# A delta-rule attention and mixture-of-experts kernel: the key products of the first two chunks over four other PSUM banks and all tiles of the array, and a planner with new prices

## The chip, the core and the metric

The kernel runs on one core of a Trainium2 chip. The metric is the device time of one execution in microseconds (us); the figure compared is the median of several executions. Five engines of the core work side by side, each through its own instructions in order: PE (TensorE, the matmuls; its weight loads are listed apart as PEld), DVE (VectorE), ACT (ScalarE), POOL (GpSimd) and SP (SyncE, which here only issues transfers). POOL issues the gathers and scatters. A result in PSUM (8 banks) can be read by DVE and ACT alone.

## The reference

```python
# attention: B=4, H=8, S=768, D=48
for t in range(S):
    y[:,:,t]  = q[:,:,t] @ state                       # read before the update
    v_old     = state^T k_n[:,:,t]                     # k_n = k/(|k|+1e-6)
    state    += beta[t] * outer(k_n[:,:,t], v[:,:,t] - v_old)
# experts: x = y laid out (4, 768, 384), 8 experts, F = 1024
logits = x @ w_gate;  local_gate = sigmoid(x @ w_local)
e      = argmax(logits) if s == 0 or local_gate < 0.5 else the expert of token s-1
out    = softmax(logits)[e] * (relu(x @ w1[e]) @ w2[e])
```

## The kernel before

**Attention** (`Attn.build`). The 768 steps are 12 chunks of 64 (`N=NCH=12`), two chunks make one of six pairs m (`NM=6`). `K(n)` loads the keys and queries of chunk n (`kq`, two tiles `KQ[g]` in two halves each, 192 KB a half) and forms the products of its keys with its keys and queries: four groups (g, c), each a function of 8 calls of `MM` into one PSUM bank out of the pool `pt`, which has two banks. A call is two records in the trace. A call takes the rows 64j and the columns 64q of the array, with q = j^c, so that one group uses two of the four 64x64 tiles. Each bank is read four times: ACT writes a part to `gt` (L208), ACT copies the same part to `G2` (L209), DVE adds another part to `gt` (L210), DVE masks the query part into `amp` (L211).

`T_(m)` turns `gt` over with DVE (L218), forms norms and scale factors in small steps (L220 to L228), scales `L` (`fL`, L232, two halves) and runs a forward substitution of 31 steps, each a product and a subtraction (L241, L242, tiles `fg` and `X`). `SPLIT=(0,0,0,0,0,0)` gives VectorE no column of it: all columns of all six substitutions are GpSimd's. Then DVE turns `X` over into `TT` (L249) and `TX` (L252).

`Tc(n)` builds the tile `XT` (pool `xtp`): ACT writes its first half (L258), copies `TT` to two bands of 32 partitions of its second half (L272, twice) and writes a second product `g2`, times -1, to the two other bands (L273). `online(n)` carries the state: products with the state into `kps` and `yps` (pools `pkp` and `pyp`, one tile of two banks each), the difference `R` (L288), the product with `XT` (`p1`), the new state (L307), the output `y` in two parts (ACT L312, DVE L313), its stores to `xs` (L317), a transposing transfer (L319) and from that the router's logits `lg` (PE L326, DVE L330).

**Experts** (`Moe`). The tokens are sorted by expert in two parts: z=0 covers chunks 0 to 9 (`SP=20` half chunks) and fills the first 256 rows of expert 0's turn, z=1 covers the rest. Routing starts at L508, gathers are L436, the up product `upm` L448, its two readers L449 and L450, the down product `downm` L455 (24 calls of 384 columns for one block of up to 128 tokens), its reader `yo` L456, the scatter L438. `weights` loads the weights of an expert in seven parts and splits each into a high half (ACT, L431) and a low half (`lo`, L433 when on DVE). `early` does so for expert 0 ahead of the routing; the tiles come from the pool `W`. `graph` is the planned part up to expert 1; `rest` writes out experts 2 to 7 in a fixed order. `CAPS=(480,496,480,448,416,384,384,384)` tokens are provided for the eight turns, so the last block of turn 3 has 64 tokens and that of turn 4 has 32.

**The order.** Everything in `build` and `graph` is given to a planner (`Sched`) as operations with what they read and write, the engines they may use and a price in ns (`c`). It ranks each by the length of the path behind it plus a bonus (`boost`, which its predecessors inherit), keeps a clock per engine, and writes one fixed instruction order for each engine. An engine of the chip then goes through that order and waits where the data are not there. So a wrong price costs no time by itself, but gives an order that waits at the wrong place.

```python
SPLIT=(0,0,0,0,0,0)                                                    # L125
H=[(j,c,j^c) for c in range(2) for j in range(2)]                      # L166
add(fm,...,e='VG'[p],c=400+2.4*n*k if p==0 else 450+3.5*n*k)           # L243, one step of a substitution
add(f,...,e='P',c=8*FT+100)                                            # L205, one group of products, FT=52
t,x=min(((c[0],c[2]) for c in cand if c[1] is o),
        key=lambda c:c[0]+(o.c[c[1]] if c[1] not in 'SI' else 0))      # L95, the engine that would end first
```

Of the kernel before, what the change touches and what calls it, by code (L numbers as in the profile page):

```python
# [120 lines left out]
class Attn:  # L121
# [37 lines left out]
    def build(s,extra=(),pre={},post=None):  # L159
# [23 lines left out]
        for f,e,c in extra: add(f,e=e,c=c,w=["consts"])  # L183

        s.kl={}; ch=[{} for _ in range(N)]; mac=[{} for _ in range(NM)]
        KV=lambda t:t.rearrange("p (u q z) t -> p u q z t",u=4,q=2)
        def K(n):

            m,cc=divmod(n,2); M=mac[m]; C=ch[n]
            KQ=C["KQ"]=[s.W(),s.W()]; am=C["am"]=s.amp(); G2=C["G2"]=s.G2()  # L190
# [158 lines left out]
class Moe:  # L349
# [545 lines left out]
```

## Time and profile before

| | |
|---|---|
| median of 3 runs | 582.48 us (582.31 to 582.53) |
| the profiled execution, its own time | 586.47 us |
| its span, first to last instruction | 584.8 us |
| PE busy | 459.1 us (79%) |
| PEld busy | 351.9 us (60%) |
| DVE busy | 329.3 us (56%) |
| ACT busy | 210.6 us (36%) |
| POOL busy | 285.9 us (49%) |
| mean granted TensorE clock | 0.842 |

The shares are averages over stages with different limits: the substitutions fill the first 267 us of POOL's time, the experts fill PE's time from about 338 us on. A row of the trace reads: start, duration, engine, line, operation, the tile written, the tile read, shapes, count, and in brackets how long the engine sat idle before it and what ended that. All times below are us from the start of the span. A granted clock of 1.00 is 2.4 GHz, one of 0.50 is 1.2 GHz.

### The profile page before, as it was taken

How to read it: one execution, taken by the hardware profiler on the slowest of the kernel's cores; microseconds unless marked ns; L12 is line 12 of the kernel's file. 1: busy time of each engine (PE TensorE's matmuls, PEld its weight loads, DVE VectorE, ACT ScalarE, POOL GpSimd, SP SyncE). 2: the span in 40 equal slices, each digit the busy share in tenths (PEclk: the TensorE clock that was granted, in tenths of full speed). 3: DMA queues.
4: the chain of work that ended last, by engine and by line, in shares of the span. 5: the costliest groups of instructions: out<-in, count | busy, mean ns of one | idle time of the engine just before them, and what ended most of it. 6: DMA issues, size and time to landing. Idle time of an engine off the chain costs nothing. (4 is left out here: it accounts for less than half of the span.)

```text
span 584.8 us, 18802 instructions
## 1 busy us (share of the span) xinstructions
PE 459.1 (79%) x8119; PEld 351.9 (60%) x8119; DVE 329.3 (56%) x722; ACT 210.6 (36%) x346; POOL 285.9 (49%) x492
## 2 busy tenths in 40 slices
PE   4660277788998887985863489999999999999992
PEld 4550267787987887885862357545565555555551
DVE  3656226547448458233486834852858685868550
ACT  2330254454644755535313211520505141426110
POOL 4089888888888897882001421032233232322301
PEclk9999999577577598586555579999999999999997
DMA  8990001624654455453056372351474656575300
GB/s 224 215 188 1 0 3 58 161 46 129 165 106 106 142 147 165 86 112 57 4 110 244 79 157 94 117 179 48 123 200 126 171 172 174 152 213 151 90 13 25
DMA packets 63668, 69.47 MB, mean 119 GB/s; under 512 B 42931, under 2 KB 54255, under 8 KB 63584
## 3 DMA queue, kind: packets, MB, share of 16 engines
q1 hardware_dynamic: 60032, 58.20, 39.6%
q0 software_dynamic: 3552, 10.06, 5.7%
q8 instruction: 64, 1.05, 0.8%
q14 instruction: 20, 0.16, 0.1%
HBM read 49.49 MB, written 10.05 MB: 102 GB/s over the span
## 5 line engine op out<-in xcount | busy, mean ns | idle before, releaser
L242 POOL TENSOR_TENSOR X<-X,fg 128x31 f32<-128x31 f32 (+15 forms) x186 | 109.8, 590 | 14.6
L241 POOL TENSOR_TENSOR fg<-L,X 128x31 f32<-128x31 f32 (+15 forms) x186 | 98.4, 529 | 16.0 <-DVE X L231 1.6
L167 PE MATMUL pt<-W 48*64 48x128 f32 x768 | 64.1, 374 | 22.6 <-DVE gt L210 13.6
L167 PEld LDWEIGHTS pt<-W 48*64 48x64 f32 x768 | 55.3, 193 | 27.3 <-DVE gt L210 16.3
L448 PEld LDWEIGHTS <-W 128*128 128x128 f16 x432 | 43.7, 102 | 33.4 <-issue 6.9
L448 PE MATMUL pt<-kv,W 128*128 128x384 f16 (+3 forms) x288 | 61.5, 346 | 0.9 <-DVE ft L450 0.7
L450 DVE TENSOR_SCALAR ft<-pt 128x384 f32<-128x384 f32 (+6 forms) x72 | 40.1, 557 | 22.6 <-ACT W L449 14.6
L167 PE MATMUL pt<-TT,G 32*32 32x32 f32 x768 | 24.3, 229 | 31.8 <-DVE TT L249 30.8
L211 DVE TENSOR_TENSOR amp<-pt,mask 128x256 f32<-128x256 f32 x48 | 20.2, 422 | 50.1 <-ACT gt L208 30.9
L449 ACT ACTIVATE W<-pt 128x256 f16<-128x256 f32 (+4 forms) x28 | 12.2, 437 | 85.5 <-PE pt L448 84.1
L167 PEld LDWEIGHTS pt<-TT,G 32*32 32x32 f32 x768 | 22.5, 139 | 33.0 <-issue 27.2
L433 DVE SCALAR_TENSOR_TENSOR W<-W,W 128x768 f16<-128x768 f32 (+1 forms) x33 | 35.9, 1093 | 10.1 <-ACT W L431 9.9
L455 PEld LDWEIGHTS <-W 128*128 128x128 f16 (+2 forms) x272 | 28.0, 103 | 21.9 <-issue 6.4
L438 POOL DMA_INDIRECT out_dram<-y,so x9 | 11.2, 1246 | 55.2 <-DVE y L456 52.8
L436 POOL DMA_INDIRECT G<-xs,gi x25 | 26.6, 1066 | 22.2 <-PE pt L612 12.6
L167 PE MATMUL kps<-R,xtp 64*64 64x48 f32 x704 | 35.6, 281 | 0.7 <-issue 0.7
L449 ACT ACTIVATE xtp<-pt 128x384 f16<-128x384 f32 (+4 forms) x28 | 14.7, 526 | 56.0 <-PE pt L448 43.9
L167 PEld LDWEIGHTS kps<-R,xtp 64*64 64x64 f32 x704 | 34.4, 200 | 0.9 <-issue 0.7
L431 ACT ACTIVATE W<-W 128x768 f16<-128x768 f32 (+1 forms) x33 | 30.2, 935 | 10.7 <-DMA W<-in_moe_w_dram 8.2
L208 ACT ACTIVATE gt<-pt,ma 128x128 f32<-128x128 f32 x48 | 22.4, 479 | 27.1 <-PE pt L167 18.6
L438 POOL DMA_INDIRECT out_dram<-kf,so x7 | 7.9, 1124 | 49.1 <-DVE kf L456 27.0
L455 PEld LDWEIGHTS <-amp 128*128 128x128 f16 (+2 forms) x224 | 22.6, 101 | 14.6 <-issue 0.9
(307 smaller groups left out, 944.1 us busy)
## 6 DMA issues: line engine op xcount, KB each, us to landing
W<-in_moe_w_dram SPq DMA_DIRECT2D x24, 512.0 KB
W<-in_moe_w_dram SPq DMA_DIRECT2D x28, 384.0 KB
W<-in_kq_dram SPq DMA_DIRECT2D x48, 192.0 KB
kv<-in_kv_dram SPq DMA_DIRECT2D x12, 768.0 KB
xs<-y SPq DMA_DIRECT2D x48, 96.0 KB
amp<-in_moe_w_dram SPq DMA_DIRECT2D x3, 384.0 KB
G<-xs,gi POOLq DMA_INDIRECT x25
kv<-G SPq DMA_TRANSPOSE x25
```

What stands on the lines that cost most here:

```text
L167: mm=lambda o,l,r,st,sp,tp:MM(o,l,r,start=st,stop=sp,skip_group_check=True,tile_position=tp)
L208: add(lambda go=go,gv=gv:nc.scalar.activation(go(),gv()[:,:,0:32],AF.Copy,scale=s.ma[:,0:1]),r=[ps,"mask"],w=[key],claim=[gt],e='A',c=ca(128))
L211: add(lambda gv=gv,n0=n0:nc.vector.tensor_tensor(am.t[:,n0:n0+4,:],gv()[:,:,64:128],s.mask.unsqueeze(1).to_broadcast([128,4,64]),op=ALU.mu ...
L241: eng.tensor_tensor(tv,l[:,j,j+1:].unsqueeze(2).to_broadcast([128,n,k]),x[:,j,x0:x1].unsqueeze(1).to_broadcast([128,n,k]),op=ALU.mult)
L242: eng.tensor_tensor(x[:,j+1:,x0:x1],x[:,j+1:,x0:x1],tv,op=ALU.subtract)
L431: if e in (None,s.nc.scalar): s.nc.scalar.mul(o,i,256.0)
L433: def wlo(s,st,w,k): s.nc.vector.scalar_tensor_tensor(s.wv(w,k)[:,1],s.wst(st,k),256.0,s.wv(w,k)[:,0],op0=ALU.mult,op1=ALU.subtract)
L436: return s.nc.gpsimd.indirect_dma_start(out=x[0:m],out_offset=None,in_=s.xs[0:nt,:],in_offset=bass.IndirectOffsetOnAxis(ap=ix[0:m],axis=0) ...
L448: for k in range(3): s.nc.tensor.matmul(ps,s.wv(W[k],k)[:,a,0,128*f:128*f+128],xT[:,3*b+k,:],start=(x==0 and k==0),stop=(x==2 and k==2))
L449: def uphi(s,h,ps): s.nc.scalar.activation(h,ps,AF.Relu,scale=2.0**-6)
L450: def upt(s,t,ps): s.nc.vector.tensor_scalar(t,ps,0.0,2.0**-6,op0=ALU.max,op1=ALU.mult)
L455: s.nc.tensor.matmul(po[0:m],h(a,f)[:,c:c+m],s.wv(W[k],k)[:,b,f%2,:],start=(x==0 and f==0),stop=(x==2 and f==7))
```

## The change

For chunks 0 and 1 the groups c=0 and c=1 of one g are one function of 16 calls in the order `H`, which goes round all four 64x64 tiles, into the two banks of `kps` (g=0) or `yps` (g=1), in place of single banks of `pt`. A one-element copy on GpSimd that reads the last tile of chunk 1 and writes the first tile of chunk 2 (`s.held`) now stands ahead of all later key loads and of all `kv` loads. VectorE's part of the experts' constants (`f3`) waits until `L` of pair 0 is scaled. The planner's prices are new. `XT`'s first half and one copy of `TT` on all partitions (in place of two on bands) may go to DVE or ACT. `Tc` and `online` get a bonus that falls with the chunk number. The low halves of four weight parts of expert 1 must be GpSimd's. The tiles of `L` and `X` join the pool `W` once the substitutions are over. In `rest`, a last block of at most 64 tokens goes to `down2`, which computes the two halves of the 384 columns on two halves of the array's columns. `SPLIT` is not touched. A few lines that only respell a list of keys are left out.

```diff
-        for f,e,c in extra: add(f,e=e,c=c,w=["consts"])
...
+            if n==2:
+                k1=ch[1]["KQ"][1]; add(lambda:nc.gpsimd.tensor_copy(KQ[0].t[0:1,0,0:1],k1.t[0:1,0,0:1]),r=[k1],w=[KQ[0]],e='G',c=200); s.held=S.ops[-1]
-                ... S.ops[-1].pre.update([s.kl[1]] if n==2 else ())
+                ... S.ops[-1].pre.update([s.held] if n>1 else ())
...
+                if n<2:
+                    bb=(s.pkp,s.pyp)[g](); bt_=bb.pool.tiles[0]; pc=[bt_[:,0],bt_[:,1]]
+                    def f(g=g,pc=pc):
+                        k=KV(KQ[g].t)
+                        for u in range(4):
+                            for j,c,q in H: mm(pc[c][B(q),128*u:128*u+128],k[D(j),u,q,0,:],k[D(j),u,q].rearrange("r z t -> r (z t)"),u==0,True,(64*j,64*q))
+                    add(f,r=[KQ[g]],w=[(bb,0),(bb,1)],claim=[bb,gt,am,G2],e='P',c=1300)
...
-                    add(f,r=[KQ[g]],w=[ps],claim=[gt,am,G2],e='P',c=8*FT+100)
+                        add(f,r=[KQ[g]],w=[ps],claim=[gt,am,G2],e='P',c=1100); s.grams.append(S.ops[-1])
+                        for o in s.outs[-8:-4]: S.links.append((o,s.grams[-1]))
...
-                    add(fm,...,c=400+2.4*n*k if p==0 else 450+3.5*n*k)
+                    add(fm,...,c=300+3.2*n*k if p==0 else 590+3.85*n*k)
-                        if j==0 and m: S.links.append((s.lastfm,S.ops[-1]))
+                        if j==0 and m>1: S.links.append((s.lastfm,S.ops[-1]))
...
-            add(lambda:nc.scalar.activation(XT.t[:,:,0:32],tt(),AF.Copy,scale=s.ma[:,0:1]),...,e='A',c=ca(512))
+            add(lambda e:e.activation(...) if e is nc.scalar else e.tensor_scalar(XT.t[:,:,0:32],tt(),s.ma[:,0:1],None,op0=ALU.mult),...,e='AV',c=dict(A=1200,V=800))
+            add(lambda e:(e.copy if e is nc.scalar else e.tensor_copy)(XT.t[:,:,32:64],tt()),r=[TT],w=[(XT,1)],claim=[XT],e='AV',c=dict(A=1070,V=700))
-                add(lambda o2=o2:nc.scalar.copy(XT.t[o2,:,32:64],tt()[o2]),r=[TT],p=[XT],e='A',c=ca(512))
...
-            add(lambda:nc.sync.dma_start(kv.t...,s.kv_[n]),w=[kv],e='S',c=786432)
+            add(lambda:nc.sync.dma_start(kv.t...,s.kv_[n]),w=[kv],e='S',c=786432); S.ops[-1].pre.add(s.held)
...
+                if m<0:
+                    for f,e,c in extra: add(f,e=e,c=c,w=["consts"]); S.ops[-1].pre.update([s.scaled] if e=='V' else ())
...
-                    Tc(n); online(n)
+                    i0=len(S.ops); Tc(n); online(n)
+                    for o in S.ops[i0:]: o.boost=2000.*(N-n)
-        for pool in (s.amp,s.xtp):
+        for pool in (s.L,s.X,s.amp,s.xtp):
             s.W.join(pool,[[o for b in pool.bufs for o in b.ops]]*len(pool.tiles))
...
+    def down2(s,po,h,W,c,m,y,pv):
+        for f in range(8):
+            k=3+f//2
+            for x,(a,b) in enumerate(((0,0),(0,1),(1,0))):
+                for g in range(2):
+                    s.nc.tensor.matmul(po[64*g:64*g+m,0:192],h(a,f)[:,c:c+m],s.wv(W[k],k)[:,b,f%2,192*g:192*g+192],...,tile_position=(0,64*g))
+        s.nc.scalar.copy(y[0:m,192:384],po[64:64+m,0:192])
+        s.nc.vector.tensor_scalar(y[0:m,0:192],po[0:m,0:192],pv[0:m],2.0**-26,op0=ALU.mult,op1=ALU.mult)
+        s.nc.vector.tensor_scalar(y[0:m,192:384],y[0:m,192:384],pv[0:m],2.0**-26,op0=ALU.mult,op1=ALU.mult)
...
-            add(lo,...,e='VG',c=dict(V=cv(n),G=2*cg(n)))
+            add(lo,...,e='G' if aft and k>2 else 'VG',c=dict(V=cv(n),G=2*cg(n)))
...
-                s.downm(po,lambda z,f:h(z,f,n),W[e],range(8),128*j,m)
-                s.yo(y,po,s.pv[:,a:a+1],m); s.scatter(y,s.so[:,a:a+1],m)
+                if m>64:
+                    s.downm(po,lambda z,f:h(z,f,n),W[e],range(8),128*j,m); s.yo(y,po,s.pv[:,a:a+1],m)
+                else: s.down2(po,lambda z,f:h(z,f,n),W[e],128*j,m,y,s.pv[:,a:a+1])
+                s.scatter(y,s.so[:,a:a+1],m)
```

## Rows read from the trace of the kernel before

**Rows 1.** The timeline of POOL: start, duration, engine, line, operation, out<-in with shapes, count, idle time before it and what ended that. POOL's copy ahead of the first substitution, the first step of the first substitution and the last step of the sixth.

```profile
27.80 0.76 POOL L231 COPY X<-mm 128x32 f32<-128x32 f32 x1 [19.20 <-DVE mm L226]
...
28.65 0.52 POOL L241 TENSOR_TENSOR fg<-L,X 128x31 f32<-128x31 f32 x1
...
267.08 0.25 POOL L242 TENSOR_TENSOR X<-X,fg 128x31 f32<-128x31 f32 x1
```

**Rows 2.** Busy time by stretch: from:to, length, then busy time (and count of instructions) of PE, PEld, DVE, ACT and POOL, then granted clock, DMA share, GB/s. The stretches are the carried state after the last substitution, expert 0's first products, and everything from there to the end.

```profile
267.30:300.00 32.70, 29.23 (x917) 27.98 (x918) 15.96 (x49) 15.14 (x19) 0.03 (x1) 0.50 0.27 52
...
316.00:338.00 22.00, 10.72 (x108) 7.84 (x108) 17.86 (x50) 7.78 (x12) 7.46 (x6) 0.50 0.41 105
...
338.00:585.00 247.00, 224.94 (x1421) 133.74 (x1418) 146.62 (x255) 69.80 (x111) 59.27 (x51) 0.98 0.45 129
```

**Rows 3.** The timeline of all engines from the first products of chunk 0 to the scale factors of pair 0. PE's rows of 32 (or 30) records are two groups of products.

```profile
5.14 2.88 PE L167 MATMUL pt<-W 48*64 48x128 f32 x30 [0.34 <-DMA W<-in_kq_dram]
...
7.19 1.28 ACT L208 ACT_TABLE_LOAD   x1 [7.19 <-PE pt L167]
...
10.33 3.07 PE L167 MATMUL pt<-W 48*64 48x128 f32 x32 [2.30 <-DVE gt L210]
...
12.35 0.48 ACT L208 ACTIVATE gt<-pt,ma 128x128 f32<-128x128 f32 x1 [1.45 <-PE pt L167]
...
12.86 0.42 DVE L211 TENSOR_TENSOR amp<-pt,mask 128x256 f32<-128x256 f32 x1 [1.48 <-ACT gt L208]
...
13.61 0.43 DVE L210 SCALAR_TENSOR_TENSOR gt<-pt,ma,gt 128x128 f32<-128x128 f32 x1 [0.33 <-ACT G L209]
...
14.10 3.13 PE L167 MATMUL pt<-W 48*64 48x128 f32 x32 [0.70 <-DVE gt L210]
...
14.45 0.27 ACT L209 COPY G<-pt 128x128 f32<-128x128 f32 x1 [0.49 <-DVE amp L211]
...
14.74 0.46 DVE L210 SCALAR_TENSOR_TENSOR gt<-pt,ma,gt 128x128 f32<-128x128 f32 x1 [0.33 <-ACT G L209]
...
21.69 3.12 PE L167 MATMUL pt<-W 48*64 48x128 f32 x32 [0.68 <-DVE gt L210]
...
22.81 1.42 DVE L218 STREAM_TRANSPOSE L<-gt 128x256 f32<-128x256 f32 x4
...
24.27 0.19 DVE L220 TENSOR_SCALAR ss<-L 128x32 f32<-128x32 f32 x1
...
24.38 0.18 DVE L395 CAST io<-ib 128x54 f32<-128x54 int32 x1
...
24.49 0.23 ACT L221 ACTIVATE s<-ss 128x32 f32<-128x32 f32 x1 [0.69 <-DVE ss L220]
...
25.88 0.35 DVE L222 RECIPROCAL t<-s 128x32 f32<-128x32 f32 x1
```

**Rows 4.** The timeline of PE in the stretch with granted clock 0.50: the product with `XT`, which uses two tiles of the array, and a product with the state, which uses all four, 64 records of 48 columns each.

```profile
277.63 3.65 PE L167 MATMUL kps<-R,xtp 64*64 64x48 f32 x64
...
273.81 1.96 PE L167 MATMUL yps<-S,W 48*64 48x48 f32 x64
```

**Rows 5.** Transfers at the start: the busy row of the stretch 5.00 to 14.60 (columns as in rows 2) and SP's first issue of `kv` loads.

```profile
5.00:14.60 9.60, 6.46 (x68) 5.66 (x70) 2.85 (x7) 3.94 (x9) 2.99 (x31) 1.00 1.03 268
...
6.14 2.45 SPq L274 DMA_DIRECT2D kv<-in_kv_dram  x3
```

**Rows 6.** POOL and DVE side by side around 125 us, and two groups of instructions (xcount | busy, mean ns of one | idle before): DVE's small scaling steps while POOL works, and the band copies of ACT that write `XT` from `TT`.

```profile
124.21 0.62 POOL L241 TENSOR_TENSOR fg<-L,X 128x256 f32<-128x256 f32 x1
...
125.72 1.23 POOL L241 TENSOR_TENSOR fg<-L,X 128x255 f32<-128x255 f32 x1
...
125.29 1.17 DVE L276 TENSOR_TENSOR kv<-kv,nT 128x768 f32<-128x768 f32 x1
...
L220 DVE TENSOR_SCALAR ss<-L 128x32 f32<-128x32 f32 x5 | 1.7, 340 | 0.2
...
L272 ACT COPY xtp<-TT 32x512 f32<-32x512 f32 x24 | 25.9, 1078 | 0.4
```

**Rows 7.** The timeline after the last substitution: the end of chunk 9's output (ACT, then DVE), what DVE does between, the start of routing for z=0, and PE on expert 0.

```profile
261.85 0.81 ACT L312 ACTIVATE y<-yps 128x768 f16<-128x768 f32 x1 [0.66 <-PE yps L167]
...
267.36 0.45 DVE L249 STREAM_TRANSPOSE TT<-X 128x256 f32<-128x256 f32 x1 [7.25 <-POOL X L242]
...
270.52 0.96 DVE L313 SCALAR_TENSOR_TENSOR y<-yps,y 128x768 f16<-128x768 f32 x1
...
286.26 0.32 DVE L508 TENSOR_REDUCE mxl<-lg 128x20 f32<-128x160 f32 x1
...
338.02 4.59 PE L448 MATMUL pt<-W,W 128*128 128x256 f16 x36
...
342.56 0.49 PE L444 MATMUL pt<-mident,Us 128*128 128x128 f16 x6
...
345.83 9.54 PE L455 MATMUL pt<-W,W 128*128 128x384 f16 x48 [1.72 <-ACT W L639]
...
355.20 1.90 PE L448 MATMUL pt<-W,W 128*128 128x224 f16 x18
```

**Rows 8.** The timeline of PE: the first records of the last block of turn 3 (64 tokens), and the first of what follows it.

```profile
463.90 0.51 PE L455 MATMUL yps<-amp,xtp 128*64 128x384 f16 x2
...
467.92 0.53 PE L448 MATMUL pt<-kv,X 128*128 128x416 f16 x2
```

More of the change, by code (lines that the diff above doesn't have):

```diff
@@ L182, in build @@
         add(wsp,r=["wc0","wc1"],w=["wc"],c=300)
-        for f,e,c in extra: add(f,e=e,c=c,w=["consts"])
-        s.kl={}; ch=[{} for _ in range(N)]; mac=[{} for _ in range(NM)]
+        s.kl={}; s.grams=[]; s.outs=[]; ch=[{} for _ in range(N)]; mac=[{} for _ in range(NM)]
         KV=lambda t:t.rearrange("p (u q z) t -> p u q z t",u=4,q=2)
@@ L211, in K @@
-                    add(lambda gv=gv,n0=n0:nc.vector.tensor_tensor(am.t[:,n0:n0+4,:],gv()[:,:,64:128],s.mask.unsqueeze(1).to_broadcast([128,4,64]),op=ALU.mult),r=[ps,"mask"],p=[am],c=cv(256)+50)
+                    add(lambda go=go,gv=gv:nc.scalar.activation(go(),gv()[:,:,0:32],AF.Copy,scale=s.ma[:,0:1]),r=[ps,"mask"],w=[key],claim=[gt,*cl],e='A',c=480)
+                    add(lambda gv=gv,n0=n0:nc.scalar.copy(G2.t[:,n0:n0+4,:],gv()[:,:,0:32]),r=[ps],p=[G2],claim=cl,e='A',c=ca(128))
+                    add(lambda go=go,gv=gv:nc.vector.scalar_tensor_tensor(go(),gv()[:,:,32:64],s.ma[:,1:2],go(),op0=ALU.mult,op1=ALU.add),r=[ps,"mask",key],p=[gt],claim=[gt,*cl],c=450)
@@ L232, in fL @@
             def fL(e,z): l=full(L.t)[:,16*z:16*z+16]; e.tensor_mul(l,l,mu.t.unsqueeze(1).to_broadcast([128,16,32]))
-            for z in range(2): add(lambda e,z=z:fL(e,z),r=[mu,ss],w=[(L,z)],claim=[L],**VG(512))
+            for z in range(2): add(lambda e,z=z:fL(e,z),r=[mu,ss],w=[(L,z)],claim=[L],**VG(512)); s.scaled=S.ops[-1]
             for j in range(31):
@@ L603, in graph @@
             add(fv,r=["tb"+Z,"smr"+Z,CK],w=["va"+Z],c=600)
-            r0,r1=(0,SP) if z==0 else (0,NS); nn=r1-r0; obk=[("ob",i) for i in range(0,r1,4)]; oak=["oa0"] if z==0 else ["oa1","oa2"]
+            r0,r1=(0,SP) if z==0 else (0,NS); nn=r1-r0; obk=[("ob",i) for i in [*range(0,SP,4),*range(SP,r1,4)]]; oak=["oa0"] if z==0 else ["oa1","oa2"]
             for part,(c0,c1,vk) in enumerate(((0,3,[]),(3,5,["va0"]+(["va1"] if z else [])))):
@@ L627, in graph @@
                 if part==0: add(fin2,r=["gi"+Z],w=["so"+Z],c=600)
+            if z==0:
+                for o_ in S.ops[iz_:]: o_.boost=0.
             i_=len(S.ops)
@@ L674, in graph @@
         add(lambda:s.oneh(4,8,ta,rhv()),r=["ta","va0","va1",CK],w=[rh],c=900)
-        add(lambda:s.prods(4,8,rhv(),q.t),r=[rh]+[("ob",i) for i in range(0,NS,4)],w=[q],claim=[OB,OB2],e='P',c=24*50)
+        add(lambda:s.prods(4,8,rhv(),q.t),r=[rh]+[("ob",i) for i in [*range(0,SP,4),*range(SP,NS,4)]],w=[q],claim=[OB,OB2],e='P',c=24*50)
         add(lambda:s.finish(4,8,q.t,tq[2]),r=[q],w=["gi2"],c=1500)
@@ L693, in graph @@
         add(lambda:s.oneh(8,20,ta,r2()),r=["ta","va0","va1",CK],w=[rh2],c=2100)
-        add(lambda:s.prods(8,20,r2(),q2.t),r=[rh2]+[("ob",i) for i in range(0,NS,4)],w=[q2],claim=[OB,OB2],e='P',c=24*50)
+        add(lambda:s.prods(8,20,r2(),q2.t),r=[rh2]+[("ob",i) for i in [*range(0,SP,4),*range(SP,NS,4)]],w=[q2],claim=[OB,OB2],e='P',c=24*50)
         add(lambda:s.finish(8,20,q2.t,s.tx),r=[q2],w=["gi3"],c=1500)
@@ L730, in rest @@
         P=lambda pool:list(pool.tiles)
[L731 removed]
+        i2=[t is s.X2.t for t in P(A.kv)].index(True); s.xT2=[P(A.kv)[i2],P(A.kv)[(i2+1)%3]]; s.hq4=[b.t for b in s.hh1]; s.hx4=[b.t for b in s.hx_]; s.spare=P(A.TT)[1:]+[P(A.kv)[(i2+2)%3]]
         used=[b.t for b in s.W2]
```

42 lines of the change are left out of this document (22 added, 20 removed).

## Prediction

> **What bounds the kernel now.** I read the page's busy slices first, then the engine timelines and the busy time by stretch; the page's chain of waits is of no help, since it holds only the last scatter. Three stages follow one another.
>
> From 27.80 to 267.33 GpSimd is the bound: its copy at 27.80 ends an idle time of 19.20 us, the first step starts at 28.65, and the sixth substitution's last step ends at 267.08 + 0.25 [rows 1]. These 238.7 us hold hardly a wait; what starts GpSimd earlier moves everything behind it.
>
> From 267.30 to 338 GpSimd is nearly idle and a chain of latencies runs: state of chunks 10 and 11, routing, expert 0's first products. TensorE's granted clock is 0.50 there, its level of 1.2 GHz. It is busy 29.23 of the first 32.70 us and only 10.72 of the last 22.00 [rows 2].
>
> From 338 to the end TensorE is the bound: 224.94 of 247 us busy at a granted clock of 0.98 [rows 2]. Matmul time taken out there, or moved ahead of 338, is saved.
>
> **The start.** Now two groups of products take 3.07 us [rows 3]. A bank's four reads alternate between ACT and DVE: ACT 12.35, DVE 12.86, ACT, DVE 13.61 to 14.04; then products may refill that bank (14.10). The second bank's last read ends at 14.74 + 0.46 = 15.20, so one g (two banks) takes 2.85 us to read out, and ACT is free for the next g at 14.45 + 0.27 = 14.72, 2.37 us after it began [rows 3]. Four such rounds end at 22.81, where DVE turns `gt` over [rows 3].
>
> After: the new function makes 32 records on four tiles. No row shows these products so; the nearest pair is 64 records of 48 columns, 3.65 us on two tiles and 1.96 on four [rows 4], a ratio of 0.54, so 3.07 becomes 1.65. First g: 5.14 to 6.79. Its readers still wait for ACT's table load, 7.19 + 1.28 = 8.47 [rows 3]. With 2.85 us for one g and 2.37 between starts: g1 is read 8.47 to 11.32, g2 10.84 to 13.69. The third g needs the first pair of banks, so its products run 11.4 to 13.05, its reading 13.5 (0.45 from product to reader: now half of 3.07 after 10.33 is 11.87, and the reader starts at 12.35) to 16.35. The fourth needs the second pair: products 13.75 to 15.40, reading 15.85 to 18.70. That replaces 22.81: **4.1 us**. Bounds: with products as slow as now (3.07) the last reading ends at 20.85, which leaves 2.0; with DVE alone as the limit, two reads of 0.42 and two of 0.46 a g, it ends at 8.47 + 4 x 1.76 = 15.5, which gives 7.3. I take 4.1 because the reading order above is the one that the rows show.
>
> The Trainium skill, TensorEngine Tiling (Array Packing), Performance Considerations, says that tiling speeds up TensorE but not the emptying of PSUM, which may become the bottleneck. By that rule alone four readings in a row, 4 x 2.85 behind 8.47, would end at 19.9 and give an estimate of 2.9; the alternation in the rows agrees with it, and the two extra bank pairs soften it.
>
> From 22.81 to 27.80 the norms are formed. The square root ends at 24.49 + 0.23 = 24.72, but the reciprocal starts at 25.88, because DVE does the 12 small operations of `f3` from 24.38 on [rows 3]. Put behind `fL` they run while GpSimd substitutes: **1.1 us**. Start together: **-5.2 us**, between -3.1 and -8.4.
>
> The transfers and the copy that holds them cost nothing. Chunk 0 and 1 are 1.57 MB; at 268 GB/s [rows 5] that is 5.9 us, so the last half lands near 11 us, ahead of the fourth products at 13.75. Behind the copy wait, on GpSimd, the copy that starts the substitution (now near 22.6) and, on SP, the `kv` and later key loads, which now begin at 6.14 [rows 5] and then near 12. Chunk 2's products start at 21.69 today [rows 3], but pair 1 is wanted only when the first substitution ends, 38 us after it began; without that cover each us of delay would count in full.
>
> **The substitutions.** `SPLIT` is zero before and after, so GpSimd's 186 step pairs stay as they are; the new price only changes what the planner thinks. What can change is DVE beside them. A step of 255 elements takes 1.23 us where the one before, of 256, takes 0.62: DVE's product of 768 elements, 1.17 us, runs beside it [rows 6], so GpSimd loses 0.61. After, each chunk's two `XT` operations from `TT` may go to DVE; the planner takes the engine that would end first, and its prices favour DVE (800 and 700 against 1200 and 1070). For chunks 0 to 9 these are up to 20 operations of 512 elements beside GpSimd. No row shows one. Below, they cost nothing; above, as much as the row with two inputs, 20 x 0.61 = 12.2. The small one-input steps of L220 take 340 ns on average while GpSimd works and 0.19 us while it is idle [rows 3, 6], so one-input operations do meet GpSimd. I scale by elements, 0.61 x 512/768 = 0.41, and give DVE half of them: 10 x 0.41 = **+4.1 us**.
>
> The Trainium skill, GPSIMD Engine Reference, Specifications, states that GpSimd shares its SBUF interfaces with VectorE and contends with DVE instructions that have two SBUF inputs or run in a 2-port mode. The two-input rows agree; whether these copies are of the second sort no row shows, and if they are, the third rival below is its result.
>
> **The tail.** DVE waits 7.25 us, to 267.36, for the last substitution, with chunk 9's output queued behind it: ACT's part of `y` ends at 261.85 + 0.81, DVE's starts only at 270.52. All of z=0 hangs on it: routing starts at 286.26, and expert 0's first half still does its last up products at 338.02 (4.59 us) and its down products at 345.83 (9.54 us) [rows 7]. The old price put a substitution's 31 steps (sum of n*k 5,456) at 31 x 0.45 + 3.5 x 5.456 = 33.0 us, the new at 31 x 0.59 + 3.85 x 5.456 = 39.3; the six really take 238.7/6 = 39.8 each [rows 1]. A planner that believes the true length should put chunk 9's output ahead of the turn-over of the last `X`. The direct wait is 7.25 us. The most that can come of it: all the first half's 4.59 + 9.54 = 14.1 us of products done ahead of 338, where TensorE is idle half the time. Nothing, if another wait takes its place. I take the wait itself, **-7.3 us**. `Tc` saves ACT one band copy of 1.08 us per chunk [rows 6] and expert 1's low halves leave DVE for an idle GpSimd; I count both inside the -7.3.
>
> **The experts.** A last block of turn 3 takes 463.90 to 467.92, 4.02 us [rows 8], for 64 tokens; turn 4's, with 32 tokens, has the same 24 calls. With two column halves at the ratio 0.54: 2 x 4.02 x 0.46 = **-3.7 us**; nothing if the halves do not overlap, 4.0 if wholly. `down2`'s extra ACT copy and DVE operation hide behind the next up products (72 calls), since four banks take turns; uncovered they are about 1 us each.
>
> **Sum.** -5.2 + 4.1 - 7.3 - 3.7 = -12.1. The profiled execution took 586.47, so 574.4; it stands 3.99 above the median of 582.48, so the median becomes **570.4 us**.
>
> **Rivals.**
> 1. The order gains nothing in the tail: a wait on TensorE or ACT takes the place of DVE's. For it: 29.23 of 32.70 us of TensorE are busy there already. -5.2 + 4.1 - 3.7 = -4.8: 577.7.
> 2. The order is right throughout: expert 0's first half is done early (14.1) and DVE's copies do not touch GpSimd. -5.2 - 14.1 - 3.7 = -23.0: 559.5. For it: 18.5 us lie between the end of ACT's `y` and the routing that needs it, beyond a few us of transfer. Against: TensorE's 0.50 clock.
> 3. Slower: all 20 `XT` operations sit on DVE and each costs GpSimd 0.61, and the tail gains nothing: -5.2 - 3.7 + 12.2 = +3.3: 585.8. It decides from 8.9/20 = 0.45 us each on; with the tail's gain, only from 0.81, which is more than the row.
> 4. The tiles do not do what they say: four are no faster than two, and column halves run one after the other. -3.1 + 4.1 - 7.3 = -6.3: 576.2.
>
> **Chances.** Forecast 0.45 (565 to 576), rival 1 0.17, rival 2 0.21, rival 3 0.10, rival 4 0.07. A range from 558 to 582 leaves out most of rival 3 and the far side of rival 2. A change of 0.2%, 1.2 us, is about what can be told from none: above 583.6 is rival 3 (slower, 0.09), the edges of rivals 1 and 3 give 0.04 for the same, the rest is faster, 0.87.
>
> **What would show it.** GpSimd's first step near 23.4 instead of 28.65; products of 1.65 us that write `kps` and `yps`; no `f3` between square root and reciprocal; the last substitution ending near 266; chunk 9's `y` on DVE ahead of the last `TT`; routing well ahead of 286; blocks of 64 and 32 tokens in 2.2 us. Wrong would be: substitutions much longer than 39.8 us, with DVE writing `xtp` beside them; or the same expert start relative to the last substitution.

## The result: 0.77% slower, where 2.1% faster was forecast

| | before | after |
|---|---|---|
| median of six runs each | 582.81 us (582.31 to 584.11) | 587.78 us (586.32 to 589.98) |
| ratio, 95% interval | | 1.0077 [1.0059, 1.0095] |
| profiled execution, and its span | 586.47, 584.8 us | 588.24, 586.5 us |
| mean granted TensorE clock | 0.842 | 0.814 |

The forecast was 570.4 us (558 to 582). The profiled execution of before lies 3.7 us above its median, that of after 0.5 above. So the two traces differ by 1.7 us in span where the medians differ by 5.0. Ratios below are always to the kernel before on the same chip.

The two spans are compared in four pieces. The borders are GpSimd's last substitution step, the start of the routing of z=1 (which needs the logits of chunk 11), and turn 2's first up product:

| piece | before | after | difference |
|---|---|---|---|
| to the end of the last step | 267.33 | 273.46 | +6.13 |
| from there to the routing of z=1 | 40.94 | 45.79 | +4.85 |
| from there to turn 2 | 96.80 | 91.19 | -5.61 |
| from there to the end | 179.73 | 176.06 | -3.67 |

Some 2.5 us of the -5.61 belong to this one execution of before: experiment 4 below, whose order is that of before up to turn 2, has 94.35 us in that piece.

Two of the borders in before, from its timelines:

```profile
308.27 0.18 DVE L508 TENSOR_REDUCE mxl<-lg 128x4 f32<-128x32 f32 x1
...
405.07 1.18 PE L448 MATMUL pt<-kv,W 128*128 128x480 f16 x5
```

### The profile page after: what moved, and what is told of

Same layout as the page of the kernel before. It is cut to its first block, busy times and chain, and to the rows that moved or that the text cites. A ratio compares the mean times of both kernels' runs of the same rounds, so it can differ in the third digit from the quotient of the medians.

```text
span 586.5 us, 18892 instructions
## 1 busy us (share of the span) xinstructions
PE 461.6 (79%) x8167; PEld 358.2 (61%) x8167; DVE 337.2 (57%) x724; ACT 189.8 (32%) x330; POOL 303.2 (52%) x503
## 5 line engine op out<-in xcount | busy, mean ns | idle before, releaser
L257 POOL TENSOR_TENSOR X<-X,fg 128x31 f32<-128x31 f32 (+15 forms) x186 | 110.6, 595 | 14.6
L256 POOL TENSOR_TENSOR fg<-L,X 128x31 f32<-128x31 f32 (+15 forms) x186 | 97.6, 525 | 25.1 <-DVE X L246 10.3
L167 PE MATMUL pt<-W 48*64 48x128 f32 x640 | 53.2, 378 | 15.1 <-DVE gt L224 7.9
L167 PEld LDWEIGHTS pt<-W 48*64 48x64 f32 x640 | 46.2, 196 | 18.8 <-ACT G L223 9.9
L473 PEld LDWEIGHTS <-W 128*128 128x128 f16 (+2 forms) x364 | 36.3, 100 | 22.7 <-issue 0.2
L466 PEld LDWEIGHTS <-W 128*128 128x128 f16 x336 | 34.0, 102 | 24.0 <-issue 5.9
L467 ACT ACTIVATE amp<-pt 128x384 f16<-128x384 f32 (+5 forms) x36 | 17.6, 490 | 79.2 <-PE pt L466 62.6
L167 PE MATMUL yps<-S,W 48*64 48x48 f32 x704 | 19.9, 290 | 24.0 <-DVE y L328 23.9
L167 PEld LDWEIGHTS yps<-S,W 48*64 48x64 f32 x704 | 18.4, 205 | 25.6 <-DVE y L328 25.5
L454 POOL DMA_INDIRECT G<-xs,gi x25 | 28.1, 1125 | 10.3 <-issue 7.3
L467 ACT ACTIVATE W<-pt 128x384 f16<-128x384 f32 (+5 forms) x36 | 17.8, 495 | 44.2 <-PE pt L466 33.5
L451 DVE SCALAR_TENSOR_TENSOR W<-W,W 128x768 f16<-128x768 f32 (+1 forms) x24 | 26.3, 1096 | 6.8 <-ACT W L449 6.8
L466 PE MATMUL pt<-kv,xtp 128*128 128x416 f16 (+2 forms) x96 | 29.0, 342 | 0.5 <-DVE ft L468 0.4
```

The lines of the kernel that those rows point to most:

```text
L167: mm=lambda o,l,r,st,sp,tp:MM(o,l,r,start=st,stop=sp,skip_group_check=True,tile_position=tp)
L256: eng.tensor_tensor(tv,l[:,j,j+1:].unsqueeze(2).to_broadcast([128,n,k]),x[:,j,x0:x1].unsqueeze(1).to_broadcast([128,n,k]),op=ALU.mult)
L257: eng.tensor_tensor(x[:,j+1:,x0:x1],x[:,j+1:,x0:x1],tv,op=ALU.subtract)
L451: def wlo(s,st,w,k): s.nc.vector.scalar_tensor_tensor(s.wv(w,k)[:,1],s.wst(st,k),256.0,s.wv(w,k)[:,0],op0=ALU.mult,op1=ALU.subtract)
L454: return s.nc.gpsimd.indirect_dma_start(out=x[0:m],out_offset=None,in_=s.xs[0:nt,:],in_offset=bass.IndirectOffsetOnAxis(ap=ix[0:m],axis=0) ...
L466: for k in range(3): s.nc.tensor.matmul(ps,s.wv(W[k],k)[:,a,0,128*f:128*f+128],xT[:,3*b+k,:],start=(x==0 and k==0),stop=(x==2 and k==2))
```

## The profile after

GpSimd's timeline, which answers to [rows 1]: the copy ahead of the first substitution, the first steps of the first, fourth, fifth and sixth, and the last step.

```profile
24.78 0.76 POOL L246 COPY X<-mm 128x32 f32<-128x32 f32 x1 [15.16 <-DVE mm L241]
25.98 0.24 POOL L256 TENSOR_TENSOR fg<-L,X 128x31 f32<-128x31 f32 x1 [0.44 <-POOL X L246]
...
144.79 0.53 POOL L256 TENSOR_TENSOR fg<-L,X 128x31 f32<-128x31 f32 x1 [3.70 <-DVE X L246]
...
189.55 0.25 POOL L256 TENSOR_TENSOR fg<-L,X 128x31 f32<-128x31 f32 x1 [6.43 <-DVE X L246]
...
232.29 0.53 POOL L256 TENSOR_TENSOR fg<-L,X 128x31 f32<-128x31 f32 x1 [0.20 <-DVE X L246]
...
273.21 0.25 POOL L257 TENSOR_TENSOR X<-X,fg 128x31 f32<-128x31 f32 x1
```

The first step comes 2.67 us earlier than at 28.65. Then GpSimd stands still 3.70 + 6.43 + 0.20 = 10.33 us, each time for the factors of the next pair. The page's groups of steps (xcount | busy, mean ns | idle before, releaser) show that the sum of the work is the same: 110.6 + 97.6 = 208.2 us. Before they held 109.8 + 98.4 = 208.2, with 1.6 us of such waits.

```profile
L257 POOL TENSOR_TENSOR X<-X,fg 128x31 f32<-128x31 f32 (+15 forms) x186 | 110.6, 595 | 14.6
L256 POOL TENSOR_TENSOR fg<-L,X 128x31 f32<-128x31 f32 (+15 forms) x186 | 97.6, 525 | 25.1 <-DVE X L246 10.3
```

What was late ahead of 144.79 is seen on the other engines: the second key products of the pair on PE, their readers on ACT and DVE, the turn-over, the factors.

```profile
131.01 2.22 PE L167 MATMUL pt<-W 48*64 48x128 f32 x26
...
133.00 0.48 ACT L222 ACTIVATE gt<-pt,ma 128x128 f32<-128x128 f32 x1 [0.93 <-PE pt L167]
...
133.51 0.42 DVE L225 TENSOR_TENSOR amp<-pt,mask 128x256 f32<-128x256 f32 x1 [10.41 <-ACT gt L222]
...
139.53 1.42 DVE L233 STREAM_TRANSPOSE L<-gt 128x256 f32<-128x256 f32 x4
...
144.46 0.19 DVE L246 COPY X<-mm 128x32 f32<-128x32 f32 x1
```

The products begin 27 us into a substitution that lasts 37 (103.70 to 141.09). From there to the factors it takes 13.5 us. DVE has stood 10.41 us at the reading of a bank that PE had not yet filled, with everything of its order behind it.

The start, which answers to [rows 3]: products of one g, and the first reader of each of the last three g's.

```profile
11.36 0.49 ACT L222 ACTIVATE gt<-yps,ma 128x128 f32<-128x128 f32 x1
11.52 1.99 PE L167 MATMUL kps<-W 48*64 48x128 f32 x32 [2.73 <-ACT G L223]
...
14.61 0.49 ACT L222 ACTIVATE gt<-kps,ma 128x128 f32<-128x128 f32 x1
...
17.86 0.49 ACT L222 ACTIVATE gt<-yps,ma 128x128 f32<-128x128 f32 x1
...
20.92 1.42 DVE L233 STREAM_TRANSPOSE L<-gt 128x256 f32<-128x256 f32 x4
```

Four tiles make the 32 records in 1.99 us in place of 3.07. But a g is read out in 3.25 us, and the next does not begin before it is done.

The tail, which answers to [rows 7]: chunk 9's output, the turn-over, the routing of z=0, its last DVE result that the counting products need, those products, the routing of z=1, turn 2.

```profile
276.43 0.96 DVE L328 SCALAR_TENSOR_TENSOR y<-yps,y 128x768 f16<-128x768 f32 x1 [3.58 <-ACT y L327]
...
278.16 1.42 DVE L264 STREAM_TRANSPOSE TT<-X 128x256 f32<-128x256 f32 x4
...
283.03 0.32 DVE L536 TENSOR_REDUCE mxl<-lg 128x20 f32<-128x160 f32 x1
...
290.00 0.16 DVE L567 CAST tl<-kf 128x8 f16<-128x8 f32 x1
...
300.98 0.32 PE L570 MATMUL pt<-oh,tri 128*128 128x160 f16 x1
...
319.25 0.19 DVE L536 TENSOR_REDUCE mxl<-lg 128x4 f32<-128x32 f32 x1
...
410.44 0.37 PE L466 MATMUL pt<-kv,W 128*128 128x480 f16 x1
```

DVE's wait of 7.25 us for the last substitution is gone, and chunk 9's output stands ahead of the turn-over. Routing of z=0 starts 9.6 us behind the last step (18.9 before). Yet its counting products wait 10.8 us (290.16 to 300.98) on PE behind chunks 10 and 11, and the routing of z=1 comes 11 us later than before.

The last block of turn 3, which answers to [rows 8]: 469.29 to 471.39, 2.10 us in place of 4.02.

```profile
469.29 0.36 PE L480 MATMUL yps<-amp,amp 128*64 128x192 f16 x4
...
471.39 0.53 PE L466 MATMUL pt<-kv,xtp 128*128 128x416 f16 x2
```

## Experiments: which part costs what

Each kernel's ratio, and from its trace: GpSimd's waits for DVE between the first and the last step (for the factors of a pair, or for the tile `X` that GpSimd clears ahead of one), the end of the last step, the start of the routing of z=1, and turn 2 (all us).

| kernel | ratio [95%] | waits | last step | z=1 | turn 2 |
|---|---|---|---|---|---|
| before | 1 | 1.6 | 267.3 | 308.3 | 405.1 |
| after | 1.0077 [1.0059, 1.0095] | 10.3 | 273.5 | 319.3 | 410.4 |
| 1 before, new step price | 1.0487 [1.0461, 1.0514] | 34.8 | 296.9 | 342.8 | 432.3 |
| 2 after, old product price | 1.0253 [1.0231, 1.0274] | 17.6 | 283.8 | 330.1 | 421.2 |
| 3 after, three old prices | 1.0088 [1.0068, 1.0109] | 0 | 265.9 | 315.1 | 410.2 |
| 4 before, split down block | 0.9922 [0.9901, 0.9942] | 2.0 | 267.7 | 307.9 | 402.2 |
| 5 after, counts first | 1.0097 [1.0061, 1.0133] | 11.5 | 274.6 | 325.3 | 415.9 |
| 6 before, start | 0.9941 [0.9916, 0.9965] | 2.5 | 264.5 | 308.1 | 400.4 |
| 7 after, product price 1450 | 1.0035 [1.0003, 1.0067] | 10.8 | 277.8 | 315.2 | 412.8 |
| 8 the same, step 480 + 3.6 | 0.9964 [0.9935, 0.9993] | 3.8 | 271.3 | 312.7 | 406.7 |
| 9 before, start and split block | 0.9857 [0.9826, 0.9888] | 2.5 | 264.2 | 308.2 | 402.8 |
| 10 third, no bonus | 0.9952 [0.9927, 0.9976] | 1.6 | 266.9 | 308.8 | 405.2 |
| 11 third, XT on ACT | 1.0087 [1.0055, 1.0119] | 5.3 | 267.0 | 316.3 | 412.7 |
| 12 ninth, product price 1100 | 1.0099 [1.0064, 1.0133] | 14.2 | 272.7 | 320.4 | 413.5 |
| 13 ninth, new XT | 0.9947 [0.9924, 0.9969] | 0.3 | 266.5 | 308.1 | 402.2 |
| 14 ninth, joined tiles, lows | 1.0093 [1.0074, 1.0111] | 1.0 | 263.4 | 305.1 | 410.6 |
| 15 ninth, bonus | 1.0088 [1.0072, 1.0103] | 8.1 | 268.8 | 318.2 | 413.3 |
| 16 ninth, lows on GpSimd | 1.0033 [1.0012, 1.0055] | 6.0 | 266.8 | 308.6 | 409.0 |
| 17 after, lows on VectorE | 1.0028 [1.0009, 1.0047] | 11.7 | 274.1 | 320.2 | 407.9 |
| 18 ninth, joined tiles | 0.9860 [0.9838, 0.9883] | 1.5 | 263.3 | 305.0 | 395.7 |

**1: the step price alone.**

```diff
-c=400+2.4*n*k if p==0 else 450+3.5*n*k
+c=300+3.2*n*k if p==0 else 590+3.85*n*k
```

> The kernel before with one line changed: the planner's price of a substitution step, 590 + 3.85 nk in place of 450 + 3.5 nk. No instruction is added or removed; only the order can differ. Theory A (the price did it: believing a substitution to last 39 us and not 33, the planner puts more of the attention's work on TensorE, VectorE and ScalarE ahead of the next pair's key products, and GpSimd then waits for them): GpSimd's waits ahead of a substitution's first step rise from 1.6 us to 6 to 11 us, the last step ends 4 to 9 us later than 267.3, time 585 to 589 us. Theory B (the new price of a group of products and the links behind the read-outs did it): the waits stay under 3 us, time 582 to 584 us. Theory C (the later loads did it: the held copy): the same as B.

Measured: 4.9% slower without one instruction more. The sign is theory A's; the waits of 34.8 us and the time lie far above its ranges. The waits (us in total, times, longest):

```profile
POOL fg L241 <- DVE X L231: 34.8, 3, 13.7
```

Theory A holds in its mechanism: the price alone makes GpSimd wait. (B falls in experiment 2. C falls in 3 and 6, where the held copy stays and GpSimd waits 0 and 2.5 us.) Believing a substitution to be longer, the planner puts more work beside each one. The third substitution begins at 105.9 in the kernel before and at 105.8 in this one; the key products of chunk 7 follow at 130.38 there, ahead of a state update (`Sps`), and at 142.65 here, behind it (first row before, the others here):

```profile
130.38 2.23 PE L167 MATMUL pt<-W 48*64 48x128 f32 x26
...
141.33 1.53 PE L167 MATMUL Sps<-Us,kv 64*48 64x48 f32 x64
142.65 2.22 PE L167 MATMUL pt<-W 48*64 48x128 f32 x26
```

On the chip that work also takes longer than its prices (a product `f1` is priced 1.66 us and takes 2.0 at 184.13; two groups of key products are priced 1.03 and take 2.89 at 176.40), so the next pair's factors come late. Under the old price the step was too cheap as well (33.0 us a substitution where 39.8 are real), so that the two errors went together.

**2 and 3: old product price, three old prices.**

```diff
-e='P',c=1100); s.grams.append(S.ops[-1])
-                        for o in s.outs[-8:-4]: S.links.append((o,s.grams[-1]))
+e='P',c=8*FT+100); s.grams.append(S.ops[-1])
```

The third also takes back the step price (above) and the four readers' prices.

> The changed kernel with the price of a group of key products back at 8*52 + 100 ns and without the links from read-outs to products; the new step price stays. Theory A: GpSimd's waits stay at 7 to 13 us, time 585 to 590 us. Theory B: they fall to under 3 us, the last substitution ends near 265 us, time 577 to 581 us. Theory C: as the changed kernel, 586 to 589 us.

> The changed kernel with three prices of before: a step of the substitution, a group of key products (and no links), and the four read-outs. Start, held copy, XT's engines, joined tiles and the split down block stay. Theories A and B: GpSimd waits under 3 us behind the first step, which starts near 26.0; the last step ends at 264 to 266 us; the tail goes back to the late order of before (routing some 19 us behind the last step); the time is 582.8 - 2.7 (start) - 3.7 (down blocks) = 576.4, between 574 and 579 us. Theory C: waits stay at 8 to 11 us, 585 to 589 us.

The second got worse, not better, and lies outside all three ranges: the new product price, with its links, softens the step price's harm, and theory B falls. In the third the waits are gone and the first step starts at 24.13, but the time (576.4 expected) is no better than the changed kernel's, and no theory had that: there the wait has moved. DVE turns `X` over before chunk 6's output, and PE stands 13.29 us for the bank that this output must empty (two views, DVE then PE):

```profile
226.04 0.45 DVE L263 STREAM_TRANSPOSE TT<-X 128x256 f32<-128x256 f32 x1 [5.25 <-POOL X L256]
...
229.23 0.91 DVE L327 SCALAR_TENSOR_TENSOR y<-yps,y 128x768 f16<-128x768 f32 x1
...
230.19 1.96 PE L167 MATMUL yps<-S,W 48*64 48x48 f32 x64 [13.29 <-DVE y L327]
```

**4, 6 and 9: the parts that change instructions, alone and together.** Four is `down2` for blocks of at most 64 tokens in the kernel before; six is the new function for chunks 0 and 1, the held copy and `f3` behind `fL`, all at old prices; nine is both.

```diff
+                else: s.down2(po,lambda z,f:h(z,f,n),W[e],128*j,m,y,s.pv[:,a:a+1])
...
+                if n<2: bb=(s.pkp,s.pyp)[g](); ...
+                    ... for j,c,q in H: mm(pc[c][B(q),...],...)
+                    ... add(f,...); S.ops[-1].pre.update([s.scaled] if e=='V' else ())
```

> The kernel before with the split down block alone (down2 for the last block of turns 3 and 4). My step: 2 x 4.02 x 0.46 = 3.7 us less, 579.1 us, between 578.8 and 580. Rival: the block is shortened but the next up products wait instead (for the readers or the weights): 582 to 583 us.

> The kernel before with the start alone: four-tile products of chunks 0 and 1 into kps and yps, the held copy and later loads, the constants' VectorE part behind the scaling of L; all old prices, bands of XT on ScalarE, old down block. First step of GpSimd between 23.5 and 26.0 us in place of 28.65. My prediction's reading (what starts GpSimd earlier moves everything behind it): last step 2.7 to 4.5 us earlier than 267.3, time 578 to 580 us. Rival F (the order of TensorE and VectorE, not GpSimd's start, sets the end; moving one end of the plan reshuffles the rest): last step earlier, but the time anywhere from 580 to 590 us.

> The kernel before with the two parts that gained alone, the start (ratio 0.9941 to before) and the split down blocks (0.9922), all prices of before. If the two lie in different stages they add: 0.9941 x 0.9922 = 0.9863, 8.0 us less than before, 574.8 us where before is 582.8. Rival: the earlier start is eaten again by the wait for chunk 11, so that only one of the two counts: 0.992 to 0.994.

All three came close to what the first theory said, and they add: 0.9941 x 0.9922 = 0.9863, measured 0.9857. The first and last step of the sixth:

```profile
24.14 0.24 POOL L254 TENSOR_TENSOR fg<-L,X 128x31 f32<-128x31 f32 x1 [0.45 <-POOL X L244]
...
264.25 0.25 POOL L255 TENSOR_TENSOR X<-X,fg 128x31 f32<-128x31 f32 x1
```

The last step comes 2.8 us earlier in the sixth, but the routing of z=1 only 0.1 (308.14 against 308.27). So the earlier start does not move everything behind it: in before, 4, 6, 9, 13 and 16 the last step ends anywhere from 264.2 to 267.7 us and the routing of z=1 starts from 307.9 to 308.6. What holds it there stays open. The sixth has its gain behind that point (92.2 us to turn 2, 94.35 in experiment 4). It routes z=0 1.8 us earlier (284.47 against 286.26); that this is the reason is likely, but no run shows it alone.

**5: the routing of z=0 earlier.** Two edges for the planner:

```diff
+                for o_ in (A.tf1,A.tp3): o_.pre.add(S.ops[-1])
```

> The changed kernel with one pair of edges more for the planner: chunk 10's state update (p3) and chunk 11's first product (f1) come behind the counting products of the routing of z=0 in TensorE's order. In the changed kernel these counting products have their data at 290.1 us and start at 300.98, behind eight blocks of chunks 10 and 11. Theory D (this queue is the second loss): they start near 292, the first gather near 304 to 306 in place of 314.7, and the total falls by 5 to 9 us, 579 to 583 us. Rival E (what is moved ahead only delays chunk 11, whose routing is then later by as much, and the experts wait for that or for the weights): total within 2 us of the changed kernel, 586 to 589 us. GpSimd's waits stay at 10 us under both.

The counts start at 293.41, the first gather at 305.47 in place of 314.74, and nothing is gained: the routing of z=1 moves from 319.3 to 325.3. Rival E holds. In the table turn 2 follows the routing of z=1 by 88 to 98 us in all kernels but 14 and 16 (105.5 and 100.4, below), whenever z=0 was routed. The spread of 10 us says that the routing of z=1 is the larger part of what turn 2 waits for, not the whole.

**7, 8 and 12: other prices.** Seven sets the product price to 1450; eight also the step price to 480 + 3.6 nk; twelve sets 1100 in the ninth.

```diff
-e='P',c=1100); s.grams.append(S.ops[-1])
+e='P',c=1450); s.grams.append(S.ops[-1])
...
-590+3.85*n*k
+480+3.6*n*k
```

> The changed kernel with one number changed: a group of key products is priced at 1450 ns in place of 1100 (the trace has two groups in 2.89 us). Theory A, said as a ratio (a step priced at its length and products priced too low, against each other): with both near their length GpSimd's waits fall from 10.3 to under 4 us, the last step ends near 266 to 269 us, time 578 to 584 us. Rival: the step price alone is at fault, whatever the products' price: waits stay over 8 us, 585 us and more.

> The changed kernel with the product price 1450 and the step price 480 + 3.6 nk (between the old and the new one). Theory A: GpSimd waits under 4 us, last step at 263 to 267 us, attention's chunk 9 no later than in the changed kernel, time 572 to 579 us. Rival (the step price is a knob without a right side, the gain of one order is chance): 583 to 590 us.

> The ninth kernel with the product price 1100 in place of 516 ns (no links), the step price old. Theory A as a ratio (products dearer against steps: they are put earlier): GpSimd's waits under 2 us as in the ninth; the rest of the attention later or not at all later; 0.978 to 0.990. Rival: any move of one price away from the set of before costs several us: 0.992 to 1.005.

Seven is not clear of the changed kernel (the intervals overlap), and goes its rival's way: GpSimd waits 10.8 us, now at the copy for the fourth substitution. Eight differs from seven in the step price alone: the waits fall from 10.8 to 3.8 us and the ratio from 1.0035 to 0.9964. So the step price makes waits in the changed kernel too, at that product price at least; yet eight misses its time (some 581 us, 572 to 579 expected) and its last step. In twelve a product price nearer to the trace costs 2.4% and raises the waits from 2.5 to 14.2 us, against the sign of theory A as a ratio and beyond its rival's range. So the ratio explains the direction of experiment 1, but predicts no order: each price changes many places at once.

**10, 11, 13, 15: bonus and XT.**

```diff
-                    for o in S.ops[i0:]: o.boost=2000.*(N-n)
```

Ten takes this line out of the third, fifteen puts it into the ninth. Eleven gives XT back to ScalarE in the third, thirteen gives XT's new operations (`e='AV'`) to the ninth.

> The changed kernel with the three old prices (as in the third experiment, 1.0088) and also without the bonus on Tc and online. Still in it against the ninth: XT's engines, the joined tiles, the low halves on GpSimd. Theory G (under old prices the bonus is what makes the order bad: ahead of chunk 9's output the rest of its pair is drawn forward): 0.985 to 0.996, chunk 11's routing near 308 us in place of 315. Rival H (it is XT's choice of engine): no change, 1.006 to 1.011.

> The changed kernel with the three old prices and XT written by ScalarE alone, as before (first half, two band copies); bonus, joined tiles and the low halves on GpSimd stay. Theory H (XT's engines and prices make the order bad): 0.985 to 0.996. Theory G (the bonus): 1.003 to 1.011. VectorE's XT operations cost GpSimd 0.7 us in the changed kernel, so under neither does GpSimd's own busy time move by more than 1 us for that reason.

> The ninth kernel (start and split down blocks, 0.9857) with XT's new operations: first half and the copy of TT on VectorE or ScalarE, with their prices. Tells where the 0.95% between the tenth kernel (0.9952) and the ninth went. Theory: the planner's order moves with XT's prices, 0.990 to 1.000; as a cost to GpSimd alone (0.7 us in all) it would stay at 0.985 to 0.988.

> The ninth kernel with the bonus 2000 x (12 - n) on Tc and online and nothing else. Theory G (under old prices the bonus spoils the order, as between the third kernel, 1.0088, and the tenth, 0.9952): 0.995 to 1.012. Rival (the bonus is bad only together with XT's new prices): 0.984 to 0.990.

Theory G holds twice: under old prices the bonus costs 1.4% (3 against 10) and 2.3% (15 against 9); the routing of z=1 moves by 6 and 10 us. XT's new operations change the time by nothing in the third (11 against 3) and cost 0.9% in the ninth by the medians; the two profiled executions do not show where (spans of 578.8 and 578.1 us). At the new prices no run takes the bonus out; the order that the planner writes there without it differs in the place of one transfer's issue alone, so it is not a cause.

What XT on VectorE does to GpSimd is seen at the old prices. The groups of steps sum to 108.2 + 99.4 = 207.6 us in the ninth and 112.4 + 99.8 = 212.2 in the thirteenth, with seven XT operations of VectorE beside them; to 207.2 in the eleventh and 212.6 in the third, with five. The same step of 112 elements beside the same clearing of `X`, in the ninth and, with an XT copy behind that, in the thirteenth:

```profile
65.63 0.43 POOL L255 TENSOR_TENSOR X<-X,fg 128x112 f32<-128x112 f32 x1
...
65.59 1.59 POOL L255 TENSOR_TENSOR X<-X,fg 128x112 f32<-128x112 f32 x1
...
65.58 0.91 DVE L243 MEMSET X<- 128x1024 f32 x1 [0.28 <-DVE TX L265]
66.41 0.47 DVE L283 COPY xtp<-TT 128x512 f32<-128x512 f32 x1
```

So the 0.7 us that the expectations of 11 and 13 name is too little: it is some 5 us there. In the third it is made up, since the eleventh waits 5.3 us for factors and the third for none. In the thirteenth the last step comes 2.3 us later than in the ninth, but the routing of z=1 does not.

**14, 16, 17, 18: the tail's two edits.**

```diff
-e='G' if aft and k>2 else 'VG'
+e='VG'
...
+for pool in (s.L,s.X,s.amp,s.xtp):
```

Seventeen makes the first edit in the changed kernel. Sixteen makes the opposite one in the ninth (the low halves must be GpSimd's), eighteen makes the second there, fourteen has both the joined tiles and the low halves on GpSimd.

> The ninth kernel with the tiles of L and X joined to the pool W and the low halves of expert 1's last four parts on GpSimd. Nothing before the routing moves. Theory: on an idle engine and with more tiles it costs nothing, 0.984 to 0.987. Rival: a low half takes about twice as long on GpSimd as on VectorE, and expert 1 waits for it: 0.988 to 0.995.

> The ninth kernel with expert 1's last four low halves on GpSimd and nothing else. In the fourteenth, which has them and the joined tiles, VectorE's subtraction that makes the low half of expert 0's hidden values (128x256) takes 1009 ns on average, in the ninth 425 ns, beside GpSimd's work. Theory I (GpSimd's low halves slow VectorE, which is the bound of that stage): the subtraction near 700 to 1000 ns while they run, ratio 0.992 to 1.010. Rival J (the joined tiles do it): 0.984 to 0.988.

> The changed kernel with the low halves free to go to either engine again (the planner then puts all on VectorE). Theory I: the hidden values' subtraction falls from 1056 to near 430 ns, up products of turn 2 start 4 to 8 us earlier than 410.4, ratio 0.994 to 1.001 where the changed kernel has 1.0077. Rival J: 1.004 to 1.010.

> The ninth kernel with the tiles of L and X joined to the pool W and nothing else. Theory I: 0.984 to 0.988. Rival J (the tiles let weight loads and their splitting come earlier and stand in the way): 0.992 to 1.010.

The joined tiles alone are free (0.9860), the low halves on GpSimd cost 1.8% of the ninth and 0.5% of the changed kernel. Seventeen gains less than theory I had it (turn 2 comes 2.5 us earlier, not 4 to 8), and fourteen lies above both of its ranges: with the low halves there, the joined tiles cost another 0.6% (1.0093 against 1.0033), and why is open. The cause of the 1.8% is in the groups of VectorE: expert 0's subtraction, in the ninth and in the sixteenth, and GpSimd's low halves beside it.

```profile
L671 DVE TENSOR_TENSOR W<-ft,W 128x256 f16<-128x256 f32 x8 | 3.4, 425 | 0.3
...
L671 DVE TENSOR_TENSOR W<-ft,W 128x256 f16<-128x256 f32 x8 | 7.8, 979 | 0.7 <-ACT W L464 0.4
...
L496 POOL TENSOR_TENSOR amp<-amp,amp 128x768 f16<-128x768 f32 x3 | 5.4, 1793 | 0.2
```

The 979 ns are an average of two sorts. Four of the eight, beside no product of GpSimd, take 0.42 to 0.43 us as in the ninth; the other four, beside its products of 768 elements, take 1.24 to 2.07. One of each in the sixteenth, and a product of GpSimd:

```profile
340.45 0.43 DVE L671 TENSOR_TENSOR W<-ft,W 128x256 f16<-128x256 f32 x1
...
341.44 2.07 DVE L671 TENSOR_TENSOR W<-ft,W 128x256 f16<-128x256 f32 x1
...
341.74 1.47 POOL L496 TENSOR_TENSOR amp<-amp,c 128x768 f32<-128x768 f32 x1
```

PE's longest wait there, for expert 0's reader, goes from 6.4 us (ninth) to 11.8 (sixteenth):

```profile
PE pt L742 <- DVE ft L465: 6.4, 1, 6.4
...
PE pt L742 <- DVE ft L465: 11.8, 1, 11.8
```

## Why the prediction was wrong, point by point

**The step that failed** is the sentence "what starts GpSimd earlier moves everything behind it", together with "the new price only changes what the planner thinks". The first holds at old prices as far as the last step, not up to the routing of z=1 (6: last step 2.8 us earlier, z=1 0.1 us, 0.59% faster). But what the planner thinks is the order, and the order alone moved the time by 4.9% (1). In the changed kernel GpSimd's waits, which the sum put at no change, rose from 1.6 to 10.3 us: -2.7 + 8.7 = +6.0 of the +6.1 at the last step. The prediction saw the new price and looked for its effect in the tail alone.

**The start.** -5.2 was forecast, -2.7 measured, -4.5 in the sixth. Constants: 1.1 as forecast (22.81 to 27.80 before, 20.92 to 24.78 after); 0.35 of it is lost again between GpSimd's copy and its first step (1.20 us in place of 0.85). Products: 1.99 us, not 1.65. The readers' order decides the rest: 2.37 us between two g's were assumed, the old readers' prices give 2.67 (6), the new ones 3.25. The Trainium skill, TensorEngine Tiling (Array Packing), Performance Considerations, says that the emptying of PSUM may become the bottleneck. The trace agrees: the next products wait for ACT's last read (2.73 us at 11.52), and the readings' gain is 1.9 us in the changed kernel against the estimate of 2.9.

**XT on VectorE.** +4.1 was forecast from ten operations at 0.41 us. The contention is real: some 5 us for five and seven operations at old prices (11 against 3, 9 against 13). In the changed kernel the planner gave VectorE 7 of 24 operations, six of them beside GpSimd's steps. Steps beside those six are together some 2.5 us longer than the shortest steps of their sizes in the runs (an estimate; the largest is a step of 207 elements at 198.83 with 1.41 us in place of 0.54). So the price of one was about right and the count too high. That the steps sum to 208.2 us before and after does not speak against it, since VectorE's other work meets fewer steps when GpSimd waits: in experiment 1, with the instructions of before and 34.8 us of waits, they sum to 204.8. Rival 3 named the right pair of engines, but not the place that cost most. There the contention came from the other side: GpSimd's low halves slow VectorE, in a stage where VectorE feeds PE. The prediction had put that edit down as a gain on "an idle GpSimd". The Trainium skill, Perfetto Trace Analysis, Optimizing Scalar/DVE Operations, warns that the two share an SBUF read port and that moving work between them may therefore not help. The trace agrees: 0.43 against 1.24 to 2.07 us in the sixteenth.

**The tail.** -7.3 was forecast from the wait of 7.25 us. That wait went, as said, and nothing was gained by it, because the tail was read from the half that does not decide. An earlier z=0 is worth nothing where z=1 comes later for it (5), and in the changed kernel the routing of z=1 starts 45.8 us behind the last step in place of 40.9. Rival 1 (no gain there, a wait on TensorE takes the place) is nearer: the counting products do wait 10.8 us on TensorE, though experiment 5 says that this wait alone is not the loss.

**The split down block.** -3.7 was forecast. Turn 3's block takes 2.10 us in place of 4.02 and turn 4's 2.09 in place of 4.00, together 3.83 us; the last piece of the span is 3.67 us shorter. Alone it is worth 0.8% (4).

**The sum.** The instructions do what was forecast: 9 is 1.4% faster, and its -8.3 us at 582.8 lie beside -5.2 and -3.7. The parts fit less well than their sum: alone the start gives 3.4 us (6) and the split block 4.5 (4). The other edits, one at a time, cost 0 to 2.4% on top of it, and the step price 4.9% on the kernel before. The readers' prices were not tried alone. The costs do not add: all together stand 2.2% above the ninth. How much of that 2.2% belongs to each price in the presence of the others stays open, because undoing one reshuffles the rest (2, 3, 7).

## What to carry to other kernels

A planner's price is a change of the program: read its effect from the order it writes, above all from what is late for the engine that bounds the stage, and expect a corrected price to harm when its neighbours stay wrong. Find the end of a tail by asking which last input the next stage cannot start without; an earlier part of the same work may be free to be late. Before moving work to an idle engine, look at the durations of the busy engine's instructions beside it.

## What the runs showed of the hardware

- A VectorE subtraction of 256 elements with two inputs takes 0.42 to 0.43 us while GpSimd forms no products and 1.24 to 2.07 us beside its products of 768 elements (sixteenth). The contention thus costs the busy engine, not only GpSimd, which loses 0.61 us in [rows 6].
- A VectorE copy with one input, of 512 elements from `TT` to `XT`, makes GpSimd's steps longer too: one of 112 elements takes 1.59 us in the thirteenth and 0.43 in the ninth.
- The granted clock says little about the end. The eighteenth kernel is among the fastest with a mean of 0.782, the kernel before has 0.842.
